# Loading q, k and v as plain rows, two-bank PSUM tiles, and transposing x pair by pair in a windowed attention followed by a soft mixture of experts

## The chip, the core and the metric

The kernel runs on one core of a Trainium2 chip. A core has five engines with instruction streams of their own: TensorE (PE in the profile; its weight loads are listed apart as PEld), VectorE (DVE), ScalarE (ACT), GpSimd (POOL) and SyncE (SP), and 16 DMA engines that move data between the chip's memory and the core's on-chip memories, SBUF and PSUM. Instructions on one engine run in order; engines wait for each other with semaphores. PSUM is where TensorE writes; it is used here in eight banks of 512 fp32 numbers per partition. The metric is device time in microseconds (us) for one execution. The kernel before took 291.89 us, the median of three runs between 289.92 and 292.55.

## The reference

Two layers, in fp32 in the reference (the kernel computes in fp16 with fp32 accumulation):

```python
# attention: q, k, v are (8 batches, 8 heads, 576 rows, 64)
scores = (q @ k.T) / 8
scores = where((0 <= i - j) & (i - j < 64), scores, -1e9)    # causal window of 64
attn   = softmax(scores)                                     # over j
x      = (attn @ v) -> transposed to (8*576 = 4608 tokens, 8*64 = 512)
# soft mixture of experts: phi (512, 8 experts * 4 slots), w1 (8, 512, 1024), w2 (8, 1024, 512)
logits = x @ phi                                             # (4608, 32)
d      = softmax(logits, over the 4608 tokens)
c      = softmax(logits, over the 32 slots)
slot_input = d.T @ x                                         # (32, 512)
slot_out   = relu(slot_input[e] @ w1[e]) @ w2[e]             # four slots per expert
out        = c @ slot_out                                    # (4608, 512), fp32
```

The expert layer can't start before all 4608 tokens have gone into `slot_input`, and the output can't start before the experts are done. So there are three stages: attention with the token side of the mixture, the experts, the output.

## The kernel before, in words

The order of all instructions is the order of the code (`manual_schedule`); tile pools add the waits for buffers. The unit of the first stage is a pair of heads of one batch: 8 x 4 = 32 pairs. The loop over `n` runs 36 times (32 pairs and `LAG` = 4), and each turn works on several pairs at different steps, so that an engine can have something from another pair:

- `st_transpose(n)`: the raw rows of q and k of pair n (tiles `qs`, `ks`) are turned on TensorE (L197, 24 transposes of 96 rows) into two banks, and ScalarE copies them to SBUF (L200), q with the scale 1/8.
- `st_score(n-3)`: a matmul with constants adds the mask and minus the row's maximum (L230, L233), matmuls add the scores (L242; the last 64 queries of each head go to a separate bank `sm`, L237 and L245), and ScalarE takes the exponential out of three banks (L248 twice, L249) into `pt`.
- `st_av(n-4)`: the weights times the values (L264, L266). Each value row has a column of ones beside it, so that the row sum comes out too. The result `av` has a two-bank PSUM tile of its own.
- `st_shift(n-2)`: the row maxima `m` are turned (L221, into the free end of `av`) and copied by VectorE to `rt` (L222), which the scores' constant matmul reads one turn later.
- `st_norm(n-4)`: VectorE takes reciprocals of the row sums (L274) and writes the normalised rows to `x_b` (L275).
- `st_max(n-1)`: the masked scores once more, with queries on the partitions (L207, L214), and VectorE's reduction to the row maxima `m` (L217), one bank per head.
- Of the batch two behind, one step per turn: in turns 0 and 1 `fr_transpose`, which turns x two pairs at a time (L291, L297; ScalarE copies, L293 and L298), in turn 2 `fr_logits` (L305; maxima, exponentials, running sums: `nb`, `lgT`, `d`, L310 to L325), in turn 3 `fr_dispatch` and `fr_slots` (`si`, L358 and L360, added to `acc`, L365). `fr_combine`, the softmax over slots, follows in the next turn (L334 to L342). The last batch's steps run one after the other behind the loop, and then the last two `fr_combine`.

PSUM holds six single banks that all steps share in turn (`bank`, pool `psum`), and the two-bank `av`.

The loads all stand in GpSimd's queue, whose instructions give the transfers to the DMA engines. At each batch's first turn: the batch's v in five transfers (L88, L90), the next batch's q and k (L79; two neighbouring rows of 64 go to one partition side by side, 96 partitions), and one expert's w1 and w2 (L62, L63). All inputs are fp32 in the chip's memory and are written to SBUF as fp16, so a row of 64 of q, k or v is 128 B when written, and two joined rows are 256 B. A value row has a pitch of 66 numbers, the ones column at 0 and the values at 1 to 64. A second copy of v, shifted by 64 rows, is made by two GpSimd copies in each batch's third turn (`shift_v`, L95, L96). A load has to wait for the last reader of the buffer that it overwrites, and the instructions behind it in GpSimd's queue wait with it. The eighth expert is loaded after the loop.

The tail: factors for the running softmax (L420 to L444), the slot inputs turned (L447, L449), the experts in two groups of four (first layer `hh` L458, transposes `th` L468, second layer `ops` L474), `osb` and `so4` (L479 to L483), then per batch five matmuls `cp` (L493) of up to 128 tokens each into one bank, copied to `ob` by ScalarE and VectorE in turn (L495, L497), and two output transfers per batch on SyncE's queue.

## Time and profile before

| | us, or as stated |
|---|---|
| median of three runs | 291.89 (289.92 to 292.55) |
| the profiled execution: span from the first to the last instruction | 285.9 |
| PE busy | 202.1 (71%), 4123 matmuls |
| VectorE busy | 142.4 (50%) |
| ScalarE busy | 133.2 (47%) |
| GpSimd busy | 99.6 (35%) |
| mean granted TensorE clock, 1 is full speed | 0.716 |
| DMA packets | 92,599, of them 75,664 under 512 B; 40.99 MB written |
| chain that ended last | PE 50%, DVE 13%, issue 10%, DMA 9%, ACT 9%, POOL 4% |

The profile is of one execution. Busy time is the time in which an engine has an instruction at work; "share" in a DMA column is the mean number of packets at work per DMA engine, so it can be above 1. In a row such as `tp<-ident_h,ks 96*64 96x96 f16 x384 | 18.9, 252 | 8.9` stand the output tile, the inputs, the shapes and how many there were; then the busy time in us, the mean of one in ns, and the idle time of the engine just before them, with what ended it. The page cuts the span into 40 slices of 7.15 us. Windows give the same for stretches that one chooses: start and end, length, then busy time and number of instructions of PE, PEld, DVE, ACT and POOL, granted clock, DMA share, and GB/s written. "The chain that ended last" is followed back from the last instruction: at each step to what released it. Its "issue" is time in which the engine waited for nothing that the profile shows.

### The profile page before, as it was taken

The page shows a single profiled execution, that of the slowest core. Times are in us where ns is not written, and L with a number is a line of the kernel's source. Part 1 is how long each engine was busy: PE and PEld are TensorE (multiplying, and loading weights), DVE is VectorE, ACT ScalarE, POOL GpSimd, SP SyncE. Part 2 cuts the span into 40 slices and gives each one's busy share as a digit, 9 for nine tenths or more (in the row PEclk, how much of TensorE's full clock was granted, in tenths as well). Part 3 has the DMA queues.
Part 4 walks back from the last instruction along what each step waited for, and adds up shares of the span by engine and source line. Part 5 has one row for each costly group of instructions (what it writes and reads, how often), then busy time and mean ns, then how long its engine had stood idle before and what let it go on. Part 6 is the DMA issues. An engine that isn't in the chain of part 4 may idle for free.

```text
span 285.9 us, 9168 instructions
## 1 busy us (share of the span) xinstructions
PE 202.1 (71%) x4123; PEld 131.1 (46%) x4123; DVE 142.4 (50%) x344; ACT 133.2 (47%) x279; POOL 99.6 (35%) x105
## 2 busy tenths in 40 slices
PE   0496875965797998599799968879866217777400
PEld 0264553743575755576475755567554003321000
DVE  4942632433663557257755537585773561155320
ACT  1353641670664466447647664583655201375210
POOL 7968127625563173509606542350020000000000
PEclk9999976695955558658855777796985555995555
DMA  7999999999999999999999999900009500029996
GB/s 75 153 134 203 192 107 196 204 113 161 210 151 133 204 178 106 187 189 99 135 205 175 108 197 196 91 5 2 2 9 190 96 1 2 0 97 338 353 333 203
DMA packets 92599, 40.99 MB, mean 143 GB/s; under 512 B 75664, under 2 KB 83856, under 8 KB 92560
## 3 DMA queue, kind: packets, MB, share of 16 engines
q0 software_dynamic: 87696, 30.97, 139.8%
q1 hardware_dynamic: 4864, 9.44, 9.8%
q8 instruction: 32, 0.52, 0.8%
q14 instruction: 7, 0.06, 0.1%
HBM read 61.93 MB, written 9.44 MB: 250 GB/s over the span
## 4 chain that ended last, share of the span: by engine, by line
PE 50%; DVE 13%; issue 10%; DMA 9%; ACT 9%; POOL 4%; DVEq 0%; POOLq 0%; ACTq 0%
PE sc L230 7%; PE tp L197 7%; PE mx L207 6%; PE av L264 6%; DMA out_dram<-ob 5%; DMA ks<-in_k_dram 5%; PE mx L214 4%; PE sc L242 3%; DVE m L217 3%; PE tx L291 2%; PE hh L458 2%; DVE ob L497 2%; PE sm L245 2%; PE av L221 2%; PE si L358 1%
## 5 line engine op out<-in xcount | busy, mean ns | idle before, releaser
L217 DVE TENSOR_REDUCE m<-mx 128x5 f16<-128x480 f32 x64 | 39.0, 652 | 8.7 <-PE mx L214 8.1
L88 POOL DMA_DIRECT2D v<-in_v_dram x32 | 28.3, 900 | 43.1 <-PE av L221 42.9
L222 DVE CAST rt<-av 10x128 f16<-10x128 f32 x32 | 9.2, 289 | 66.5 <-PE av L221 66.2
L248 ACT ACTIVATE pt<-sc 128x512 f16<-128x512 f32 x64 | 34.7, 601 | 15.3 <-PE sc L242 15.2
L200 ACT ACTIVATE qT<-tp 128x576 f16<-128x576 f16 x32 | 26.1, 816 | 24.6 <-PE tp L197 24.4
L230 PE MATMUL sc<-rt,lh 75*128 75x128 f16 x256 | 26.7, 264 | 7.3 <-issue 4.1
L207 PE MATMUL mx<-wm,ident_h 128*128 128x480 f16 x64 | 27.8, 516 | 3.0 <-issue 1.6
L200 ACT ACTIVATE kT<-tp 128x576 f16<-128x576 f16 x32 | 25.8, 805 | 7.5 <-PE tp L197 7.5
L293 ACT COPY xt<-tx 128x1024 f16<-128x1024 f16 x16 | 16.2, 1018 | 24.6 <-PE tx L291 24.6
L275 DVE TENSOR_TENSOR x_b<-av,rc 128x640 f16<-128x640 f32 x32 | 26.4, 824 | 1.1
L264 PE MATMUL av<-v,pt 128*64 128x65 f16 x576 | 21.6, 225 | 7.3 <-issue 6.6
L95 POOL COPY v<-v 64x2048 f16<-64x2048 f16 x8 | 15.2, 1906 | 32.1 <-DMA v<-in_v_dram 32.1
L197 PE MATMUL tp<-ident_h,ks 96*64 96x96 f16 x384 | 18.9, 252 | 8.9 <-DMA ks<-in_k_dram 5.0
L197 PE MATMUL tp<-ident_h,qs 96*64 96x96 f16 x384 | 19.1, 254 | 8.5 <-DMA qs<-in_q_dram 8.5
L214 PEld LDWEIGHTS <-qT 64*32 64x32 f16 x1152 | 12.3, 108 | 27.0 <-issue 26.2
L230 PEld LDWEIGHTS <-lh 75*128 75x128 f16 x256 | 19.6, 118 | 10.7 <-issue 6.0
L264 PEld LDWEIGHTS <-pt 128*64 128x64 f16 x576 | 17.0, 135 | 9.7 <-issue 7.2
L214 PE MATMUL mx<-kT,qT 64*32 64x96 f16 x1152 | 18.0, 251 | 4.1 <-issue 4.1
L197 PEld LDWEIGHTS <-qs 96*64 96x64 f16 x384 | 14.0, 141 | 13.8 <-DMA qs<-in_q_dram 8.5
L197 PEld LDWEIGHTS <-ks 96*64 96x64 f16 x384 | 15.3, 146 | 9.5 <-DMA ks<-in_k_dram 5.3
L497 DVE COPY ob<-cp 128x512 f32<-128x512 f32 (+1 forms) x20 | 12.4, 679 | 12.9 <-DMA out_dram<-ob 7.6
L318 ACT ACTIVATE d<-lg,nmax 128x128 f16<-128x128 f32 x8 | 2.9, 367 | 31.4 <-DVE lgT L314 31.4
(130 smaller groups left out, 351.4 us busy)
## 6 DMA issues: line engine op xcount, KB each, us to landing
w<-in_moe_w_dram POOLq DMA_DIRECT2D x16, 1024.0 KB, 18.5
out_dram<-ob SPq DMA_DIRECT2D x8, 1024.0 KB, 8.3
qs<-in_q_dram POOLq DMA_DIRECT2D x8, 576.0 KB, 11.5
ks<-in_k_dram POOLq DMA_DIRECT2D x8, 576.0 KB, 14.0
v<-in_v_dram POOLq DMA_DIRECT2D x32, 128.0 KB, 8.7
out_dram<-ob SPq DMA_DIRECT2D x8, 128.0 KB, 7.3
v<-in_v_dram POOLq DMA_DIRECT2D x8, 64.0 KB, 9.2
phi_sb<-in_moe_phi_dram POOLq DMA_DIRECT2D x1, 32.0 KB, 7.9
```

What stands on the lines that cost most here:

```text
L88: nc.gpsimd.dma_start(out=v1[:, :, c, 1:65], in_=v[b, :, 128 * c:128 * c + 128, :].rearrange("h p d -> p h d"))
L197: nc.tensor.transpose(tp[64 * hl:64 * hl + 64, j, GP * c:GP * c + GP], src[:, GC * (2 * hp + hl) + c, Dh * j:Dh * j + Dh], ident_h[0:GP, 0 ...
L200: nc.scalar.activation(dst.rearrange("p (g j) -> p j g", j=RQ), tp[:, :, :], AF.Copy, scale=sc)
L207: nc.tensor.matmul(mx[hl][:, :, :], ident_h[:, :], wm[:, :, :], start=True, stop=False, skip_group_check=True)
L214: nc.tensor.matmul(mx[hl][32 * t:32 * t + 32, c, :], qT[r, o:o + 32], kT[r, o:o + 96], start=False, stop=True, skip_group_check=True)
L217: nc.vector.reduce_max(m[:, 5 * hl:5 * hl + 5], mx[hl][:, :, :], axis=AXX)
L230: nc.tensor.matmul(sc[hl][:, 2 * c:2 * c + 2, :], lh[:, 5 * hl + c, :], rt[:, :], start=(c == 0), stop=False, skip_group_check=True)
L248: nc.scalar.activation(pt[:, 9 * hl:9 * hl + 8, :], sc[hl][:, :, :], AF.Exp)
L264: nc.tensor.matmul(av[r0:r0 + 64, hl, 65 * (i // 2):65 * (i // 2) + 65], pt[:, 9 * hl + i, :], rhs, start=True, stop=True)
L275: nc.vector.tensor_tensor(out=x_b[:, :, 128 * hp:128 * hp + 128].rearrange("p c (l d) -> p l c d", l=2), in0=avv[:, :, :, 1:65], in1=rc[:, ...
L293: nc.scalar.copy(out=xt[:, 2 * k2:2 * k2 + 2, 0:512], in_=tx[:, :, :])
L497: nc.vector.tensor_copy(out=ob[0:pn, t, :], in_=cp[0:pn, :])
```

## The change

The change is made all over the kernel. What is computed stays the same.

- **Loads.** q, k and v of a batch are each loaded in one transfer as plain rows: the 8 x 576 rows of a batch in order, 128 to a chunk, 36 chunks (`flat`, `NCH`). Every row is written as 128 B. Value rows now have a pitch of 96 numbers (192 B), values at 0 to 63, the ones column at 64 (`VP`). An odd head begins in the middle of a chunk. The shifted copy of v is made by VectorE, in a batch's fourth turn.
- **Order of the loads.** Ahead of the loop: q and k of batch 0 in two parts, v 0, q and k of batch 1, w1 and w2 of expert 0. Then v of the batch and q and k of the next at each batch's first turn, and one half of an expert (w1 or w2) in the turns of a list (`WSLOTS`). The eighth expert goes into the freed buffers of q and k at turn 32 (`load_last`). phi is loaded on SyncE's queue as fp32 and converted by VectorE.
- **PSUM.** Four two-bank tiles serve all steps in turn (`banks`): `tp` (q and k turned, beside them the `sm` scores and the turned dispatch weights), `sc`, `av`, `mx` and `f` (the turned x of one pair, and the logits or slot sums). One instruction empties both banks where two did before: the maxima's reduction and the large exponential.
- **x.** `fr_transpose` turns one pair per turn (five transposes, one copy) instead of two pairs in each of two turns. Logits follow in the turn after the last pair, slots one turn later.
- **fr_combine** is cut in two, one turn apart; the last one is placed among the experts.
- **Tail.** Both groups' first layers run ahead of the transposes and second layers; the output is copied from two banks at a time and sent in three transfers per batch.

The order of TensorE's work in a turn is: transposes of pair n, (dispatch transposes), scores of n-3, values of n-4, shift of n-2, maxima of n-1, (logits), x of n-5, (slots). The core of the diff:

```diff
+    NRES = E - 1
+    NCH = H * S // 128
+    VP = 96
...
-    psum = ctx.enter_context(tc.tile_pool(name="psum", bufs=6, space=bass.MemoryType.PSUM))
-    pav = ctx.enter_context(tc.tile_pool(name="pav", bufs=1, space=bass.MemoryType.PSUM))
-
-    def bank(shape, dt, name):
-        return psum.tile(shape, dt, name=name, tag="ps")
-
-
-    w1_t, w2_t = {}, {}
-
-    def load_expert(e, pool):
-        w1_t[e] = pool.tile([128, NKK, F], FP16, name=f"w1_{e}")
-        w2_t[e] = pool.tile([128, NFC, D], FP16, name=f"w2_{e}")
-        nc.gpsimd.dma_start(out=w1_t[e], in_=moe_w1[e].rearrange("(c p) f -> p c f", p=128))
-        nc.gpsimd.dma_start(out=w2_t[e], in_=moe_w2[e].rearrange("(c p) d -> p c d", p=128))
-
-    att = ExitStack()
-    pin = att.enter_context(tc.tile_pool(name="pin", bufs=2))
-    pqk = att.enter_context(tc.tile_pool(name="pqk", bufs=1))
-    pvv = att.enter_context(tc.tile_pool(name="pvv", bufs=1))
-    pw = att.enter_context(tc.tile_pool(name="pw", bufs=2))
-    pxb = att.enter_context(tc.tile_pool(name="pxb", bufs=2))
-    pxt = att.enter_context(tc.tile_pool(name="pxt", bufs=1))
+    psum = ctx.enter_context(tc.tile_pool(name="psum", bufs=4, space=bass.MemoryType.PSUM))
+    pin = ctx.enter_context(tc.tile_pool(name="pin", bufs=2))
+    def banks(name):
+        t = psum.tile([128, 2, 512], FP32, name=name, tag="ps")
+        return t, t[:, :, :].bitcast(FP16)
+    def flat(src, b):
+        return src[b].rearrange("h s d -> (h s) d").rearrange("(c p) d -> p c d", p=128)
...
-    def load_qk(b):
-        qs = pin.tile([GP, H * GC, RQ * Dh], FP16, name="qs", tag="qs")
-        ks = pin.tile([GP, H * GC, RQ * Dh], FP16, name="ks", tag="ks")
-        for t_, src in ((qs, q), (ks, k)):
-            nc.gpsimd.dma_start(out=t_, in_=src[b].rearrange("h (c g j) d -> g (h c) (j d)", g=GP, j=RQ))
...
-            nc.gpsimd.dma_start(out=v1[:, :, c, 1:65],
-                                in_=v[b, :, 128 * c:128 * c + 128, :].rearrange("h p d -> p h d"))
-        nc.gpsimd.dma_start(out=v2[64:128, :, 4, 1:65],
-                            in_=v[b, :, 512:576, :].rearrange("h p d -> p h d"))
...
-        nc.gpsimd.tensor_copy(out=v2[0:64, :, 1:5, 1:65], in_=v1[64:128, :, 0:4, 1:65])
-        nc.gpsimd.tensor_copy(out=v2[64:128, :, 0:4, 1:65], in_=v1[0:64, :, 0:4, 1:65])
...
+    def new_qk(b):
+        staged[b] = tuple(pin.tile([128, NCH, Dh], FP16, name=n, tag=n) for n in ("qs", "ks"))
+    def load_qk(b, c0=0, c1=NCH):
+        for t_, src in zip(staged[b], (q, k)):
+            nc.gpsimd.dma_start(out=t_[:, c0:c1, :], in_=flat(src, b)[:, c0:c1, :])
+    new_qk(0)
+    load_qk(0, 0, 9)
...
+    load_qk(0, 9, NCH)
...
+    def load_w(i):
+        e, second = divmod(i, 2)
+        if second:
+            nc.gpsimd.dma_start(out=w2_t[e, 0], in_=w2_dram(e))
+        else:
+            nc.gpsimd.dma_start(out=w1_t[e, 0], in_=w1_dram(e))
+    def load_last(half):
+        e = E - 1
+        a = pin.tile([128, 2, F], FP16, name="w1h", tag="qs")
+        c = pin.tile([128, 4, D], FP16, name="w2h", tag="ks")
+        nc.gpsimd.dma_start(out=a, in_=w1_dram(e)[:, 2 * half:2 * half + 2, :])
+        nc.gpsimd.dma_start(out=c, in_=w2_dram(e)[:, 4 * half:4 * half + 4, :])
+        w1_t.setdefault(e, []).extend(a[:, i, :] for i in range(2))
+        w2_t.setdefault(e, []).extend(c[:, i, :] for i in range(4))
...
+    v1s = [pvv.tile([128, NCH, VP], FP16, name=f"v1_{i}") for i in range(2)]
+    v2s = [pvv.tile([128, NCH, VP], FP16, name=f"v2_{i}") for i in range(2)]
+    def load_v(b):
+        nc.gpsimd.dma_start(out=v1s[b % 2][:, :, 0:Dh], in_=flat(v, b))
+    def shift_v(b):
+        v1, v2 = v1s[b % 2], v2s[b % 2]
+        nc.vector.tensor_copy(out=v2[64:128, :, 0:Dh], in_=v1[0:64, :, 0:Dh])
+        nc.vector.tensor_copy(out=v2[0:64, 1:NCH, 0:Dh], in_=v1[64:128, 0:NCH - 1, 0:Dh])
+    load_v(0)
+    new_qk(1)
+    load_qk(1)
+    load_w(0)
+    load_w(1)
...
+        c0 = 9 * hp
+        even = [(0, 128, c0 + c, 128 * c) for c in range(4)] + [(0, 64, c0 + 4, 512)]
+        odd = [(64, 128, c0 + 4, 0)] + [(0, 128, c0 + 5 + c, 64 + 128 * c) for c in range(4)]
+        for w, src in enumerate(staged[b]):
+            for parts in zip(even, odd):
+                for hl, (r0, r1, c, o) in enumerate(parts):
+                    nc.tensor.transpose(tq[64 * hl:64 * hl + 64, w, o:o + r1 - r0], src[r0:r1, c, :],
+                                        ident_h[r0:r1, r0:r1])
+    def st_copy(p, tq):
+        qk = qkT[p % NQ]
+        nc.scalar.activation(qk[:, 0, 64:64 + S], tq[:, 0, 0:S], AF.Copy, scale=scale)
+        nc.scalar.copy(out=qk[:, 1, 64:64 + S], in_=tq[:, 1, 0:S])
...
+        mx, _ = banks("mx")
...
+        nc.vector.reduce_max(m[:, :].rearrange("p (l c) -> p l c", l=2),
+                             mx[:, :, 0:480].rearrange("p l (c x) -> p l c x", x=96), axis=AXX)
...
+        sc, _ = banks("sc")
+        sm = tp[:, :, 288:352]
...
+    def st_exp(p, sc, sm):
+        pt = pts[p]
+        nc.scalar.activation(pt[:, :, 8, :], sm[:, :, :], AF.Exp)
+        nc.scalar.activation(pt[:, :, 0:8, :].rearrange("p l i x -> p l (i x)"), sc[:, :, :], AF.Exp)
...
+        for c in range(5):
+            n = 128 if c < 4 else 64
+            nc.tensor.transpose(fq[:, 0, 128 * c:128 * c + n], x_b[0:n, c, 128 * hp:128 * hp + 128], ident_h[0:n, 0:n])
+        nc.scalar.copy(out=xts[b][:, hp, :], in_=fq[:, 0, 0:S])
...
+        return lambda: fr_combine2(b, ec, rs, cc)
+    def fr_combine2(b, ec, rs, cc):
...
+    WSLOTS = {5: 2, 9: 3, 11: 4, 13: 5, 17: 6, 19: 7, 21: 8, 25: 9, 27: 10, 28: 11, 29: 12, 30: 13}
     LAG = 4
+    pending = {}
+    for n in range(NP + LAG + 1):
+        kb, ph = divmod(n, HP)
+        if ph == 0 and n > 0:
+            if kb < B:
+                load_v(kb)
+            if kb + 1 < B:
+                new_qk(kb + 1)
+                load_qk(kb + 1)
+        if n in WSLOTS:
+            load_w(WSLOTS[n])
+        if n == 32:
+            load_last(0)
+            load_last(1)
+        sb = (n - 10) // HP if n >= 10 and (n - 10) % HP == 0 else None
+        lb = (n - 9) // HP if n >= 9 and (n - 9) % HP == 0 else None
+        cb = (n - 11) // HP if n >= 11 and (n - 11) % HP == 0 else None
+        tp = tq = sc = None
+        if n < NP or 0 <= n - 3 < NP or sb is not None:
+            tp, tq = banks("tp")
         if n < NP:
+            st_transpose(n, tq)
+        if sb is not None:
+            fr_dispatch(sb, tq)
         if 0 <= n - 3 < NP:
+            sc, sm = st_score(n - 3, tp)
+        if n < NP:
+            st_copy(n, tq)
+        if sb is not None:
+            fr_dispatch_copy(sb, tq)
+        if sc is not None:
+            st_exp(n - 3, sc, sm)
+        av = None
+        if 0 <= n - 4 < NP or 0 <= n - 2 < NP:
+            av, _ = banks("av")
         if 0 <= n - 4 < NP:
             st_av(n - 4, av)
         if 0 <= n - 2 < NP:
             st_shift(n - 2, av)
+            st_shift_copy(n - 2, av)
         if 0 <= n - 4 < NP:
             st_norm(n - 4, av)
+        if ph == 3 and kb < B:
+            shift_v(kb)
+        if n == 5:
+            late_constants()
         if 0 <= n - 1 < NP:
             st_max(n - 1)
+        f = None
+        if 0 <= n - 5 < NP or lb is not None or sb is not None:
+            f, fq = banks("f")
+        if lb is not None:
+            lg = fr_logits(lb, f)
+        if 0 <= n - 5 < NP:
+            fr_transpose(n - 5, fq)
+        if lb is not None:
+            fr_exp(lb, lg)
+        if sb is not None:
+            si = fr_slots(sb, f)
+            fr_acc(sb, si)
+        if sb is not None:
+            pending[sb] = fr_combine(sb)
+        if cb is not None:
+            pending.pop(cb)()
...
+    f, _ = banks("f")
+    fr_exp(B - 1, fr_logits(B - 1, f))
+    tp, tq = banks("tp")
+    fr_dispatch(B - 1, tq)
+    fr_dispatch_copy(B - 1, tq)
+    f, _ = banks("f")
+    fr_acc(B - 1, fr_slots(B - 1, f))
+    pmid.close()
...
+    ha, _ = banks("ha")
+    first_layer(0, ha)
+    hb, _ = banks("hb")
+    first_layer(1, hb)
+    tht, th = banks("tht")
+    hidden_transpose(0, th)
+    finish = fr_combine(B - 1)
+    op, _ = banks("op")
+    second_layer(0, op[:, 0, :])
+    hidden_transpose(1, th)
+    second_layer(1, op[:, 0, :])
+    finish()
...
+        for t0 in (0, 2, 4):
+            cp, _ = banks("cp")
+            ts = (t0, t0 + 1) if t0 < 4 else (4,)
+            for i, t in enumerate(ts):
+                pn = 128 if t < 4 else 64
+                r = slice(32 * t, 32 * t + 32) if t < 4 else slice(96, 128)
+                o = 0 if t < 4 else 128
+                nc.tensor.matmul(cp[0:pn, i, :], ct_all[r, b, o:o + pn], so4[r, :], start=True, stop=True,
+                                 skip_group_check=True)
+            pn = 128 if t0 < 4 else 64
+            dst, src = ob[0:pn, t0:t0 + len(ts), :], cp[0:pn, 0:len(ts), :]
+            if turn % 2 == 0:
+                nc.scalar.copy(out=dst, in_=src)
             else:
+                nc.vector.tensor_copy(out=dst, in_=src)
+            turn += 1
+            if t0 < 4:
+                r0 = 576 * b + 128 * t0
+                nc.sync.dma_start(out=out[r0:r0 + 256, :].rearrange("(c p) d -> p c d", p=128),
+                                  in_=ob[:, t0:t0 + 2, :])
+            else:
+                nc.sync.dma_start(out=out[576 * b + 512:576 * b + 576, :], in_=ob[0:64, 4, :])
```

## The prediction

> **What bounds the kernel now.** I read the page first, its slices and its DMA queues:
>
> ```profile
> PEclk9999976695955558658855777796985555995555
> DMA  7999999999999999999999999900009500029996
> GB/s 75 153 134 203 192 107 196 204 113 161 210 151 133 204 178 106 187 189 99 135 205 175 108 197 196 91 5 2 2 9 190 96 1 2 0 97 338 353 333 203
> q0 software_dynamic: 87696, 30.97, 139.8%
> q8 instruction: 32, 0.52, 0.8%
> ```
>
> A slice is 7.15 us. The DMA engines are full until slice 25 (186 us), and the rate swings between about 105 and 205 GB/s. The instruction queue moves 32 packets, 0.52 MB: 16 KB each.
>
> Then the windows, the first five chosen so that one kind of load, or two that meet, can be told apart, the last one a whole batch:
>
> ```profile
> 5.00:10.00 5.00, 0.69 (x12) 0.50 (x12) 4.43 (x15) 0.76 (x1) 4.62 (x12) 1.00 1.82 181
> 108.00:113.00 5.00, 5.00 (x131) 3.28 (x127) 3.92 (x10) 2.89 (x7) 1.77 (x3) 0.82 3.96 90
> 122.00:126.00 4.00, 4.00 (x100) 2.51 (x96) 3.08 (x7) 1.04 (x3) 0.00 (x0) 0.50 1.19 207
> 179.00:182.00 3.00, 2.35 (x55) 1.74 (x56) 1.60 (x3) 1.86 (x6) 2.19 (x3) 0.91 1.93 127
> 182.00:185.00 3.00, 3.00 (x75) 1.77 (x70) 1.53 (x4) 1.51 (x4) 0.00 (x0) 0.53 2.97 77
> 105.00:131.00 26.00, 21.92 (x484) 15.72 (x478) 13.43 (x33) 14.54 (x31) 10.42 (x11) 0.65 2.09 151
> ```
>
> The last two columns are the DMA share (above 1: packets of one engine overlap) and GB/s written. q and k, 256 B written per packet, run at 181 (5:10). Weights run at 207 (122:126). v, 128 B per packet, alone in 179:185, starts at 127 and falls to 77 while the share rises from 1.93 to 2.97: its writes pile up. Where the end of v meets the next q and k (108:113) both crawl at 90 with a share of 3.96. In the batch window PE is busy for 21.9 of 26 us, DVE and ACT for 13.4 and 14.5.
>
> Then the chain that ended last, around that crawl:
>
> ```profile
> 112.73 0.54 PE mx L207 x2
> 113.28 0.23 PE mx L214 x19
> 113.51 3.73 issue
> 117.23 0.40 PE mx L214 x15
> ```
>
> PE stops in the middle of a run of equal matmuls, waiting for no other engine. Such pauses stand at 34.8 (1.66), 41.8 (4.09), 62.2 (5.64), 87.4 (1.60), 113.5 (3.73), 139.4 (2.01) and 163.1 (0.62), 19.4 us by 180: one per batch, most of them while q and k follow v. With 16 KB instruction packets on the same DMA engines I read them as late instruction fetches.
>
> So PE bounds the attention loop, with a pause per batch that the DMA crawl makes, at a clock that is often half. The first q transposes (L197) of batches 1 to 7 stand at 26.1, 49.4, 77.5, 104.5, 131.5, 155.5 and 180.3 us; the first 26 us wait for the k of batch 1. The six batches between take 154.2 us, 25.7 each.
>
> **The change, part by part.** I count from the span, 285.9 us; the median run of 291.9 is 6.0 more, which I take as fixed around the span.
>
> *Loads.* q, k and v now all come as 4608 packets of 128 B per batch and tensor, so q and k go from 2304 to 4608 packets. Values go to rows at 192 B, before at 132 B and 2 B off. A load's 0.59 MB takes 3.3 us at 181 GB/s, 4.65 us at 127, 7.7 us at 77. No row shows an aligned 128 B write alone. I take 127, what v itself does before its writes pile up: nearest in size, and without the offset, I argue, the pile need not form, since 256 B packets never piled up when alone. A weight half (1.05 MB at 207) takes 5.05 us; 1.5 of them per batch until iteration 28 instead of 2. DMA per batch: 3×4.65 + 1.5×5.05 = 21.5 us, below the 25.7 of today. POOL's queue loses the 1.9 us copies (L95, L96) and four of five v issues: DMAs only wait for PE's last use of their buffer, as before.
>
> The Trainium skill speaks against this: "DMA: Bandwidth & Descriptors", Specifications, gives 512 B as the least transfer for line rate and says that smaller ones are read-modify-written. The trace disagrees at 256 B (181 GB/s, share steady) and leaves 128 B open; by that rule the slow end of the loads, 7.7 us, would hold for q and k too. This is the third rival.
>
> *Start.* Five loads stand ahead of iteration 4: 4.0 us to the first packets (estimated from issue at 1.3 and landing at 8.5) + 5×4.65 = 27.3 against 26.1; with its first transposes 28. **+2.**
>
> *Pauses.* If the crawl goes, the pause goes: 19.4/6 = 3.2 us per batch. **−19.4.** Next late is PE itself at 22.5 us per batch, with DMA at 21.5 just under it.
>
> *PE.* 20 transposes of up to 128 columns for 24 of 96: 24×96 and 16×128+4×64 are equal columns, 1.10 us at half clock. One sm matmul fewer per pair. Pair-wise x transposes: the same 20 per batch. 0, ±0.2 us per iteration (±6).
>
> *Merged evacuations.* m 652 ns at 480 elements against nb's 362 at 192 gives 168 ns fixed, so merging saves 32×0.17 = 5.4 us of DVE; exp (601 at 512, 299 at 128) gives 198 fixed, 6.3 us of ACT. Both idle half of each window: 0, a gain only if PE ran at full clock throughout. The ring of four two-bank tiles: transposes of n+1 take the scores' tile of n, free after 0.82+0.80+0.30+1.0 = 2.9 us of ACT; PE needs 1.1+0.45+0.15+1.0+0.4 = 3.1 us at full clock (110 to 114 us in the timeline) to come back. No wait, barely.
>
> *shift_v on DVE.* Not shown in this form. lh<-mb moves 1280 in 0.67 us, lh<-db 1280 in 1.21: 2304 elements are 1.2 to 2.2 us, twice per batch. I take 2.4 in all: a plain copy, as lh<-mb. It stands ahead of the reduce that frees the tile for the next av. DVE: 0.29+0.22+0.82+2.4+1.14 = 4.9 us after av; PE returns to av after 4.9 at half clock, 3.1 at full. **+1.0 per batch, +6** (0 to +11). It also waits for v on DVE, with the reduce, and through it PE, queued behind. v is issued three iterations (17 us) ahead and lands within 10 (5.05 backlog + 4.65): covered.
>
> *Logits.* nb now also waits for ACT's copy of x (about 0.66 us) and ACT for nb; today ACT waits 31.4 us there in 8 times and PE is not held. 0 (to +5).
>
> *From iteration 28 on.* Batch 7 and the drain keep their 23.0 and 13.1 us. x^T is copied per pair: instead of 3.4 us from x_b to the last logits' start (217.1 to 220.5) about 1.7. **−1.7.** The two combines on DVE (226.06 to 231.05) leave the path: one inside the loop, one beside the experts. **−4.9.** The experts (13.3 us, 237.75 to 251.03) run as 3.6+2.6+0.5+0.85+1.9+0.4+0.85+1.9 = 12.6. **−0.7.** First output DMA after one 1.0 us copy of two banks instead of four alternating ones, 254.64 to about 253.9: **−0.7**; then 9.4 MB at about 340 GB/s as before. Expert 7's load was not on the path (hh waited for ACT's sit), so moving it wins 0; it now lands near 210, first needed after 220.
>
> Sum: +2 −19.4 +6 −1.7 −4.9 −0.7 −0.7 = −19.4; span 266.5, time **272**.
>
> **The rivals.**
> 1. *Faster: the clock stays up too.* Without pauses PE may keep full clock, where iterations took 4.1 us (161.4 to 165.5, 185.3 to 189.4). At 5.0 us a batch is 20, or 21 with the shift; DMA must keep up (3.6 us loads). 6×(25.7−21) = 28 and 3 in batch 7, plus 8: 39 off, 253. Against: 79 to 105 us ran at clock 0.50 with PE busy for 23.9 of 26 us.
> 2. *The pauses stay.* They come from any long run of small packets, of which there are now more. Batches stay at 25.7+1: +2 +6 −8 = 0: 292. The Trainium skill ("Runtime: NRT & Kernel Launch", Instruction fetch mechanics) calls fetch mostly hidden behind execution; then the pauses were never fetches and nothing here removes them. The instruction packets near each pause's end speak against it.
> 3. *Slower: 128 B is slow as such.* Place: DMA. If a load takes over 6.0 us (98 GB/s), 3 loads + 7.6 exceed 25.7 and PE waits at each batch's first transposes. At 6.6 us: batches 27.4, iteration 4 at 37: +11 +10 −8 = +13, 305. At 7.7: batches 30.7, +16 +30 −8 = +38, 330. For: 77 and 90 GB/s. Against: that v is both unaligned and small, and starts at 127.
>
> **How the numbers follow.** Forecast 0.45 (262 to 282, by the ± of PE, shift and logits); clock 0.23 (247 to 262); pauses stay 0.14 (284 to 297); 128 B slow 0.18 (295 to 330). 252 to 303 leaves out some 0.08 below and 0.12 above. One per cent is about what the three runs (289.9 to 292.6) can tell. Faster by over 1% (under 289): 0.45+0.23+0.05 = 0.73; within: 0.08; slower: 0.19.
>
> **What would show it.** Right: windows in which q and k run near 127 GB/s or above with a share near 2, DMA slices below 9 somewhere before 180 us, chain pauses ("issue") under 5 us in all, batch 7's first transposes near 168, no combine between acc and the tr matmuls. Wrong: a share of 3 to 4 through q, k and v (rival 3), transposes waiting for qs or ks in every batch, issue pauses as before (rival 2), av waiting for the reduce at each fourth iteration (shift underpriced), or a clock that falls as PE is fed less evenly.

## The result and the profile after

The changed kernel is slower: 305.22 us, the median of four runs (300.53 to 310.60), against 291.49 for the kernel before in the same runs. The ratio is 1.038, with a 95% interval of 1.029 to 1.047. Two of the four runs were slower ones at a lower granted clock, and this ratio, like all ratios below, is of the fast runs alone, so it is smaller than that of the medians. The forecast was 272. The profiled execution spans 298.8 us, 12.9 more than before.

These lines of its page answer to those shown of before (granted clock, DMA share and rate in 40 slices, now of 7.47 us; the queues of loads):

```profile
PEclk9999999998599579957995597797588555796555
DMA  8999999999599809997990999099990000008997
GB/s 62 157 147 192 189 156 171 72 156 201 97 92 158 134 2 140 171 207 56 157 178 5 135 167 213 12 154 211 208 206 12 2 0 0 3 2 306 357 355 246
q0 software_dynamic: 123584, 30.94, 123.4%
```

The DMA engines are no longer full all the time: there are slices with 5, 8 and 0, and slices at 2, 5 and 12 GB/s before the loop's end. The loads move 123,584 packets instead of 87,696, and their packets take less time in all, 123% of the engines' span instead of 140%.

Two windows: v, q and k alone, and one batch. The columns are those of the prediction, the last three granted clock, DMA share and GB/s.

```profile
36.00:44.00 8.00, 8.00 (x120) 5.23 (x118) 4.53 (x18) 3.74 (x7) 0.00 (x0) 1.00 2.53 158
111.00:138.00 27.00, 24.60 (x475) 15.55 (x472) 17.25 (x33) 13.50 (x28) 7.72 (x6) 0.81 1.75 146
```

The 128 B rows load at 158 GB/s with no crawl; 0.59 MB take 3.7 us. But PE is busy for 24.6 of 27 us, at a granted clock of 0.81, where before it was busy for 21.9 of 26 at 0.65. The loop got more TensorE work, not more waiting. Where it sits is seen in the chain that ended last: start, length, and how many matmuls. First the changed kernel, each row the whole block that turns q and k of one pair, at the slow and the fast matmul rate:

```profile
55.11 2.41 PE tp L223 x20
62.45 1.67 PE tp L223 x20
```

Then the kernel before, the same block at the fast and the slow rate:

```profile
30.93 0.79 PE tp L197 x24
40.16 1.10 PE tp L197 x24
```

Twenty transposes take twice as long as twenty-four did. The waits of TensorE (for whom, us in all, times, longest) show the other side: the pauses with no wait shown ("issue"), 20.1 us in 9 in the kernel before by the same view, are nearly gone, and a new wait stands first. Before:

```profile
PE av L264 <- issue: 6.6, 3, 5.6
PE sc L230 <- issue: 4.1, 1, 4.1
PE mx L214 <- issue: 4.1, 2, 3.7
PE tx L291 <- issue: 2.0, 1, 2.0
PE tp L197 <- issue: 1.7, 1, 1.7
PE mx L207 <- issue: 1.6, 1, 1.6
```

After:

```profile
PE tp L379 <- ACT d L348: 9.5, 8, 2.6
...
PE f L332 <- issue: 1.1, 1, 1.1
PE f L324 <- issue: 1.0, 1, 1.0
```

By stages: the first block of batch 1 stands at 26.4 us (26.1 before, though that is its k half; its q half stood at 23.3) and that of batch 7 at 193.2 (180.3), so a batch takes 27.8 us instead of 25.7. From there to the last `x_b` it is 44.5 us instead of 36.1, and from that to the end 61.1 instead of 69.5.

The starts of the matmuls in the block that begins at 62.4 us, read from the trace, in ns from the first one, with the rows that each takes (64-row ones marked h):

```
q: 0  173h  316 320  397 400  453 456  605h  749
k: 752 925h  1069 1071  1149 1152  1205 1208  1357h  1500
```

Two 128-row transposes that write to the two halves of the output partitions start 3 ns apart; the next pair follows after some 53 to 78 ns. At every step between a 128-row and a 64-row one, 143 to 173 ns pass. There are eight such steps in a block.

### The profile page after: what moved, and what is told of

Same layout as the page of the kernel before. It is cut to its first block, busy times and chain, and to the rows that moved or that the text cites. A ratio compares the mean times of both kernels' runs of the same rounds, so it can differ in the third digit from the quotient of the medians.

```text
span 298.8 us, 8723 instructions
## 1 busy us (share of the span) xinstructions
PE 236.5 (79%) x3963; PEld 142.0 (48%) x3963; DVE 160.5 (54%) x326; ACT 124.7 (42%) x245; POOL 63.6 (21%) x57
## 3 DMA queue, kind: packets, MB, share of 16 engines
q0 software_dynamic: 123584, 30.94, 123.4%
## 4 chain that ended last, share of the span: by engine, by line
PE 62%; DVE 15%; ACT 8%; DMA 6%; issue 3%; POOL 1%; DVEq 0%; SPq 0%; ACTq 0%; POOLq 0%
PE tp L223 15%; PE sc L271 7%; PE mx L236 7%; PE f L324 5%; PE av L297 5%; PE mx L243 4%; PE sc L276 4%; ACT xt L325 3%; DMA out_dram<-ob 3%; DMA ks<-in_k_dram 3%; DVE v L146 2%; PE av L251 2%; DVE m L246 2%; PE tp L263 2%; DVE x_b L309 2%
## 5 line engine op out<-in xcount | busy, mean ns | idle before, releaser
L223 PE MATMUL tp<-ident_h,qs 128*64 128x128 f16 (+1 forms) x320 | 37.1, 258 | 7.8 <-DMA qs<-in_q_dram 7.8
L228 ACT ACTIVATE qkT<-tp 128x576 f16<-128x576 f16 x32 | 20.8, 650 | 53.3 <-PE tp L267 38.7
L141 POOL DMA_DIRECT2D v<-in_v_dram x8 | 14.5, 1817 | 127.8 <-PE av L251 127.1
L325 ACT COPY xt<-f 128x576 f16<-128x576 f16 x32 | 20.4, 637 | 45.6 <-PE f L324 45.6
L223 PE MATMUL tp<-ident_h,ks 128*64 128x128 f16 (+1 forms) x320 | 37.7, 263 | 1.7 <-DMA ks<-in_k_dram 1.7
L246 DVE TENSOR_REDUCE m<-mx 128x10 f16<-128x960 f32 x32 | 36.8, 1151 | 1.6 <-PE mx L243 1.2
L285 ACT ACTIVATE pt<-sc 128x1024 f16<-128x1024 f32 x32 | 33.0, 1031 | 4.0 <-PE sc L276 2.2
L223 PEld LDWEIGHTS <-qs 128*64 128x64 f16 (+1 forms) x320 | 22.1, 121 | 21.3 <-DMA qs<-in_q_dram 8.0
L223 PEld LDWEIGHTS <-ks 128*64 128x64 f16 (+1 forms) x320 | 22.4, 123 | 12.2 <-issue 2.5
L309 DVE TENSOR_TENSOR x_b<-av,rc 128x640 f16<-128x640 f32 x32 | 26.4, 824 | 1.1
L271 PE MATMUL sc<-rt,lh 128*128 128x128 f16 x256 | 26.6, 267 | 0.2 <-ACT xt L325 0.2
L236 PE MATMUL mx<-wm,ident_h 128*128 128x480 f16 x64 | 26.2, 505 | 0.0
L229 ACT COPY qkT<-tp 128x576 f16<-128x576 f16 x32 | 20.3, 633 | 0.0
```

What stands on the lines that cost most here:

```text
L223: nc.tensor.transpose(tq[64 * hl:64 * hl + 64, w, o:o + r1 - r0], src[r0:r1, c, :], ident_h[r0:r1, r0:r1])
L228: nc.scalar.activation(qk[:, 0, 64:64 + S], tq[:, 0, 0:S], AF.Copy, scale=scale)
L236: nc.tensor.matmul(mx[:, hl, 0:480], ident_h[:, :], wm[:, :, :].rearrange("p c x -> p (c x)"), start=True, stop=False, skip_group_check=True)
L246: nc.vector.reduce_max(m[:, :].rearrange("p (l c) -> p l c", l=2), mx[:, :, 0:480].rearrange("p l (c x) -> p l c x", x=96), axis=AXX)
L271: nc.tensor.matmul(sc[:, hl, 128 * c:128 * c + 128], lh[:, 5 * hl + c, :], rt[:, :], start=(c == 0), stop=False, skip_group_check=True)
L285: nc.scalar.activation(pt[:, :, 0:8, :].rearrange("p l i x -> p l (i x)"), sc[:, :, :], AF.Exp)
```

## The experiments

### The order of the transposes

Theory: TensorE stops when the number of rows changes. Rivals: 128-row transposes are slow as such, or something else sets the pace. One edit to the changed kernel:

```diff
-        for w, src in enumerate(staged[b]):
-            for parts in zip(even, odd):
+        full = list(zip(even[0:4], odd[1:5]))
+        half = [(even[4], odd[0])]
+        for w, group in ((0, full), (1, full), (0, half), (1, half)):
+            for parts in group:
```

> The changed kernel with one edit: of the 20 transposes of q and k in a turn, the 16 that take all 128 rows come first and the four that take 64 rows last. Nothing is added or removed. In the changed kernel's trace two neighbouring 128-row transposes start 3 ns apart, but at each step between a 128-row and a 64-row one 143 to 173 ns pass; there are 8 such steps in the block, which takes 1.67 us at full clock and 2.41 at half, against 0.79 and 1.10 for before's 24. Theory, steps between row counts stop TensorE: 6 of 8 steps go, 6 x 0.11 us at full and 6 x 0.16 at half clock, so the block takes about 1.0 and 1.4, and 32 turns save 21 to 31 us of TensorE time; some of it turns into waits, so the time falls by 15 to 30 us against the changed kernel's 305. Rival 1, a 128-row transpose is slow in itself: block and time unchanged within 1%. Rival 2, VectorE (the shifted copy of v, then the reduction) or the loads set the pace: the block gets shorter but the time stays within 1% of 305.

Measured: 281.8 us, 0.976 of before (0.961 to 0.990). That is 23 us below the changed kernel by the medians, and 18 by the two ratios (0.062 of 291): the theory, and neither rival. The chain shows the block at the fast rate:

```profile
67.61 0.74 PE tp L225 x20
```

From the first to the last start the block takes 0.62 us at the fast and 1.07 at the slow rate, where it took 1.50 and 2.17: seven steps fewer inside it, 0.126 and 0.157 us each. A dose between the two, in the order `(0, full), (0, half), (1, full), (1, half)`:

> A dose between the changed kernel and a1_grouped: q's eight 128-row pairs, q's 64-row pair, then the same for k, so 3 steps between row counts inside the block of 20 transposes instead of 8 (changed kernel) or 1 (a1_grouped). From the first to the last start the block takes 1.50 us at full and 2.17 at half clock with 8 steps, 0.62 and 1.07 with one. Theory, each step costs the same, 0.126 and 0.157 us: 0.87 and 1.38 us with 3. Rival, only the pairs of unequal transposes (one of 128 and one of 64 rows) are slow, and here there are none: 0.62 and 1.07.

It takes 0.84 and 1.33 us with three steps, 0.11 and 0.13 us for each of the two added: the price is per step, within a fifth. Its one run took 282.2 us.

Next the two other places where the change had added such steps:

```diff
         for hl in range(2):
+            for c in range(4):
+                nc.tensor.matmul(sc[:, hl, 128 * c:128 * c + 128], lh[:, 5 * hl + c, :], rt[:, :],
+                                 start=(c == 0), stop=False, skip_group_check=True)
+        for hl in range(2):
             r = slice(64 * hl, 64 * hl + 64)
             nc.tensor.matmul(sm[:, hl, :], qk[r, 1, 512:640], qk[r, 0, 576:640],
                              start=False, stop=True, skip_group_check=True)
-        for hl in range(2):
-            for c in range(4):
-                nc.tensor.matmul(sc[:, hl, 128 * c:128 * c + 128], lh[:, 5 * hl + c, :], rt[:, :],
-                                 start=(c == 0), stop=False, skip_group_check=True)
...
-            n = 128 if c < 4 else 64
-            nc.tensor.transpose(fq[:, 0, 128 * c:128 * c + n], x_b[0:n, c, 128 * hp:128 * hp + 128], ident_h[0:n, 0:n])
+            nc.tensor.transpose(fq[:, 0, 128 * c:128 * c + 128], x_b[:, c, 128 * hp:128 * hp + 128], ident_h[:, :])
```

> The one before this in the list, and two more edits that take steps between row counts away: the constant matmuls of the scores come before the 64-row score matmuls of sm (three steps become one), and the fifth transpose of x takes all 128 rows instead of 64, with 64 columns that nobody reads (two steps fewer). Theory, steps stop TensorE: four more steps per turn, 4 x 0.11 to 0.16 us, less 0.03 to 0.05 for the added columns, so another 0.4 to 0.6 us per turn and 12 to 19 us of TensorE time, 8 to 18 us of the time if TensorE still sets the pace. Rival, something else bounds the turn once the block is short: no further change over 1%.

277.5 us (0.961, 0.951 to 0.971): 4.4 less, about half of what was expected, and the two intervals overlap. At the fast rate the score block does get shorter, from 1.07 to 0.86 us, and the five transposes of x from 0.33 to 0.23. But TensorE's busy time falls by 5.7 us in all (192.7 to 187.0), not by 12 to 19, and ten of its blocks of q and k stand at the slow rate, where `a1_grouped` has six; why isn't settled. TensorE waits 14.9 us in 8 times for `d` here and 5.1 for the shifted v, nearly as in `a1_grouped` (15.1 and 4.1), where the changed kernel had 9.5 and none.

The converse, planted in the kernel before:

```diff
-        for hl in range(2):
-            for c in range(4):
+        for c in range(4):
+            for hl in range(2):
                 nc.tensor.matmul(sc[hl][:, 2 * c:2 * c + 2, :], lh[:, 5 * hl + c, :], rt[:, :],
                                  start=(c == 0), stop=False, skip_group_check=True)
+            for i in (2 * c, 2 * c + 1):
+                for hl in range(2):
+                    r = slice(64 * hl, 64 * hl + 64)
+                    nc.tensor.matmul(sc[hl][:, i, :], kT[r, 64 * i:64 * i + 128], qT[r, 64 * i:64 * i + 64],
+                                     start=False, stop=True, skip_group_check=True)
...
-        for i in range(8):
-            for hl in range(2):
-                r = slice(64 * hl, 64 * hl + 64)
-                nc.tensor.matmul(sc[hl][:, i, :], kT[r, 64 * i:64 * i + 128], qT[r, 64 * i:64 * i + 64],
-                                 start=False, stop=True, skip_group_check=True)
```

> The converse, on the kernel before: the same 29 matmuls of the scores in another order, each two constant matmuls (75 rows) followed by the four 64-row score matmuls of the same columns, so 9 steps between row counts in a turn's score block instead of 1; nothing else is touched, neither loads nor PSUM. In before's trace the block takes 0.98 us at full and 1.66 at half clock from its first to its last start. Theory, a step costs 0.126 and 0.157 us wherever it stands: 8 more make the block 2.0 and 2.9 us, TensorE works 32 to 40 us more, and as it sets the pace of the loop the time rises by 20 to 35 us. Rival, the steps cost only in transposes, or only between transposes of unequal width: block and time as before, within 1%.

305.3 us (299.2 to 306.7) against 290.8 (288.3 to 294.9): 14 us more by the medians, 11 between the fastest runs, from the order of the same matmuls alone. The block takes 1.82 us at the fast and 2.57 at the slow rate, from 0.98 and 1.66: 0.105 and 0.114 us per step. PE's busy time rises from 202.1 to 239.3 us, as expected, but the time by less than the 20 expected at least: the pauses shrank from 20.1 to 8.0 us at the same time. So steps cost in ordinary matmuls too, and part of what TensorE loses shows up as shorter pauses.

### Loads

Is it the offset of v that made the crawl, and the crawl that made the pauses? The kernel before, with the value rows as in the changed one:

```diff
-    v1s = [pvv.tile([128, H, 4, 66], FP16, name=f"v1_{i}") for i in range(2)]
+    v1s = [pvv.tile([128, H, 4, 96], FP16, name=f"v1_{i}") for i in range(2)]
...
-            nc.gpsimd.dma_start(out=v1[:, :, c, 1:65],
+            nc.gpsimd.dma_start(out=v1[:, :, c, 0:64],
```

> The kernel before with one edit: value rows at a pitch of 192 B with the values at 0 and the ones column at 64, as in the changed kernel, instead of 132 B with the values 2 B off. Theory, the offset makes v's 128 B writes pile up, and the pile-up makes TensorE's pauses: v's packets then keep 150 to 160 GB/s as in the changed kernel, the share stays near 2, the pauses shrink from 19 us in all to under 5, and the time falls from 291 by 10 to 19 us. Rival, the pauses have another cause (the five small transfers, the instruction stream itself): the rate of v rises but the time stays within 1%.

273.5 us, 0.947 (0.938 to 0.955). The windows of v alone and of the q and k behind it, where before fell to 77 and 90 GB/s with a share of 3 to 4:

```profile
31.00:34.00 3.00, 3.00 (x81) 1.93 (x80) 2.03 (x5) 1.18 (x4) 0.39 (x1) 1.00 2.13 160
36.00:40.00 4.00, 2.21 (x72) 1.49 (x72) 2.46 (x5) 2.24 (x5) 2.30 (x2) 1.00 1.88 181
```

160 GB/s for v, 181 for q and k, a share near 2: the crawl came from how v's rows lay, 2 B off and at a pitch of 132 B. The edit changes both, and no run tells them apart; "offset" stands for both below. The pauses fall to 9.5 us, though not under 5. This one edit of the change, alone, is worth 15.5 us.

The other load edit alone, single rows of q and k beside the offset v (`RQ = 1` for `RQ = 2` in the kernel before):

> The kernel before with one edit: q and k as single rows, 128 B written per packet, 4608 packets per load instead of 2304; v stays at its offset. Theory, a 128 B write is not slow as such: q and k load at about 157 GB/s, 3.8 us instead of 3.3, 1 us more DMA per batch, and as loads are waited for only at the start the time stays within 1% (start +1 us). Rival, 128 B rows pile up beside weights and values whatever their place: q and k crawl at 77 to 100 GB/s, the pauses grow and the time rises by over 3%.

305.5 us, 1.058 (1.050 to 1.065): the rival, as far as time and pauses go. The windows are those in which v and the next q and k run side by side:

```profile
40.00:46.00 6.00, 4.06 (x112) 2.80 (x113) 2.98 (x7) 2.55 (x5) 1.65 (x2) 0.82 4.88 87
66.00:72.00 6.00, 1.94 (x58) 1.55 (x53) 0.72 (x2) 3.21 (x7) 1.16 (x2) 0.93 4.90 83
```

More small packets stand beside the offset rows, the share goes to 4.9, and the pauses to 31.2 us. That the offset rows slow their neighbours shows in single packets: in the kernel before, a 256 B packet of q or k takes 41 ns in the median without v (115 to 117.8 us) and 113 to 142 ns beside it (109 to 113 us), and a 128 B packet of v there 120 to 149, against 32 in `b_valign`. Both load edits together:

> The kernel before with both load edits: aligned value rows (b_valign) and q and k as single 128 B rows (b_rq1). b_rq1 alone cost 5.8% and its q and k fell to 64 to 104 GB/s beside the offset v; b_valign alone gained 5.3%. Theory, only the offset rows of v are slow, and what they slow is every small packet beside them: q, k and v all load at about 157 GB/s, 1 us per batch more than in b_valign, and the time is that of b_valign, 273, plus 0 to 4 us. Rival, single 128 B rows cost by their number whatever v does: the time is b_valign's plus 14 or more.

284.1 us (0.985, 0.973 to 0.998): 10.7 above `b_valign`, between the theory and its rival. About 5 us of it are waits for q and k, 16.9 us against 11.6 in all, mostly at the start. Single rows do cost something by their number here.

### The shifted copy of v, and the dispatch

```diff
-        if ph == 3 and kb < B:
+        if ph == 2 and kb < B:
             shift_v(kb)
```

> The kernel with all three orders mended (a2_allorder) and one edit: the shifted copy of v in a batch's third turn instead of its fourth, still on VectorE. In the traces of the changed kernel and of a2_allorder the two copies take 0.75 us each where GpSimd issues no transfer, but 1.2 and 1.97 where it issues the next v, q and k at the same time; in the fourth turn both wait for the same av, so they meet in every batch. Theory, VectorE's copies are slowed by GpSimd's issues: in the third turn both copies take 0.75 us, 1.7 us per batch less on VectorE, TensorE's wait for the copy (5.1 us in 5 times) goes, and the time falls by 6 to 14 us against a2_allorder. Rival, the copies are slow for their 64-partition shift or for the pitch: 1.2 and 1.97 us stay, and the time stays within 1%.

268.5 us (0.929, 0.912 to 0.947), 9.0 below `a2_allorder`. The two copies in the changed kernel (shortest, median, longest in ns):

```profile
L145 DVE COPY v<-v x8: 742/1167/1221, 25.3 to 220.1; 64x2304 f16<-64x2304 f16 x8
L146 DVE COPY v<-v x8: 752/1968/1970, 26.1 to 220.8; 64x2240 f16<-64x2240 f16 x8
```

and in this kernel:

```profile
L145 DVE COPY v<-v x8: 742/752/755, 18.6 to 182.0; 64x2304 f16<-64x2304 f16 x8
L146 DVE COPY v<-v x8: 752/753/1986, 19.4 to 182.8; 64x2240 f16<-64x2240 f16 x8
```

They take 0.75 us each but for one, and that one, at 19.4 us, follows another into an issue on GpSimd (L141). In the changed kernel six of eight pairs met the issues of v and of q, k or weights, because the issues wait for the last `av` that reads the buffer, and the copies stand behind the `x_b` that waits for the same `av`. Every slowed copy in these two traces ends 0.55 or 0.56 us after the end of an issue. The edit also puts the copies a turn earlier; how much of the 9.0 us comes from that and how much from their length, no run tells apart.

The Trainium skill, "SBUF — State Buffer", Who interferes with whom, says that VectorE's copies in their fast form and GpSimd's instructions share a pair of ports, and that the one that starts first blocks the other for its whole length. That fits: 0.75 us alone, 1.97 behind an issue; and at 18.6 us in `c1_shift`, where the copy took its 0.74 us inside an issue, that issue lasted 2.58 us instead of 1.82.

The dispatch transposes behind the scores, and their copies behind the exponentials:

```diff
-        if sb is not None:
-            fr_dispatch(sb, tq)
         if 0 <= n - 3 < NP:
             sc, sm = st_score(n - 3, tp)
+        if sb is not None:
+            fr_dispatch(sb, tq)
```

> The kernel a2_allorder with one edit: the transposes of the dispatch weights (td, L380 and L381) stand behind the scores in TensorE's order, and their copies behind the exponentials in ScalarE's, instead of ahead of them. In a2_allorder TensorE waits 14.9 us in 8 times there for ScalarE's d, with the scores queued behind. Theory, this wait holds the turn: inside the loop 7 x 1.8 us of it are covered by the scores (about 1.6 us at full clock), so the time falls by 5 to 12 us. Rival, the same chain over VectorE and ScalarE (copy of x, maxima, exponentials) ends last anyway and TensorE waits somewhere else in the turn: within 1%.

272.9 us (0.948, 0.936 to 0.959), 4.5 below `a2_allorder`: just under the expected range, and the intervals overlap. TensorE's wait for `d` at that place (L380) falls to 6.9 us. Both edits:

> The edits of c1_shift and c2_dispatch together on a2_allorder. Theory, they take away two different waits, one at a batch's fourth turn and one at the turn after its logits: the gains add up, 9.0 and 4.5 us off 277.5, so about 264. Rival, both give back the same slack to the same chain: no better than c1_shift's 268.5 within 1%.

264.9 us (0.924, 0.911 to 0.937): about the 264 of the theory, and 3.6 us below `c1_shift`, but the intervals overlap, so that the gains add up isn't shown beyond noise. This kernel beats both the one before and the changed one, with the changed kernel's instructions but for a few columns in the transposes of x, in another order.

### What is left of the forecast's other terms

```diff
-        nc.vector.reduce_max(m[:, :].rearrange("p (l c) -> p l c", l=2), ...
+        for hl in range(2):
+            nc.vector.reduce_max(m[:, 5 * hl:5 * hl + 5], ...
```

and the same for the exponential:

> The kernel c3_both with the merged evacuations undone: the reduction to the maxima and the large exponential one bank at a time, two instructions each again, the two-bank tiles kept. Theory of the prediction, both engines have slack: within 1%. Rival, in the turns that are left after the mended orders VectorE and ScalarE stand in the chain: 32 x 0.17 and 32 x 0.2 us come back on it, 4 to 11 us.

266.4 us (259.6 to 267.1) against 264.9 (264.6 to 268.0): no difference that these runs can tell; the rival's 11 us are excluded, its 4 not strictly. Then before's loads of q and k (two rows joined) in `c3_both`:

> The kernel c3_both with before's loads of q and k: two rows joined, 256 B per packet, 2304 packets per load, 24 transposes of 96 rows, and copies that put the rows back in order; the shifted copy of v gets a pitch of 144 B instead of 192 to make room. Theory, single rows cost by their number at the start, where the loads are waited for, and by late loads and pauses after it (b_rq1_valign stood 10.7 us above b_valign): joined rows give 4 to 10 us back against c3_both. Rival, in the loop the loads are covered and the pauses were already gone in the changed kernel (16 us of gaps on TensorE from 25 to 230 us, two of them with no wait shown): only the start moves, by 1 to 4 us, and ScalarE's copies, 0.81 us for 0.64, take it back: within 1%.

263.2 us (0.913, 0.896 to 0.929) against 0.924: 1.7 us, within 1%, so the rival. TensorE's waits for q and k are 11.6 us instead of 15.0. Why single rows cost 10.7 us in the older order of work and hardly anything here isn't settled.

Last, the pauses, which come back in `c3_both`: 16.0 us in 10, with no crawl. Two kernels leave loads out, the first those of q, k and v from batch 2 on, the second the weights' too, but for the first and the last expert (its last hunk).

```diff
-            if kb < B:
+            if kb == 1:
                 load_v(kb)
             if kb + 1 < B:
-                new_qk(kb + 1)
-                load_qk(kb + 1)
+                staged[kb + 1] = staged[(kb + 1) % 2]
...
-        if n in WSLOTS:
-            load_w(WSLOTS[n])
```

> The kernel c3_both without the loads of q, k and v from batch 2 on: later batches compute on the data of batches 0 and 1 that are still in place, so the output isn't the reference's; all else, the weights' loads too, stays. By the waits with no releaser on TensorE the pauses are 20.1 us in the kernel before, 9.5 in b_valign, 2.1 in the changed kernel, 8.0 in b_steps and 16.0 in c3_both: they shrink with the crawl, but also wherever TensorE is slower. Theory, small packets on the DMA engines delay the instruction fetch: without them the pauses fall under 5 us. Rival, TensorE in the short turn takes its instructions faster than they come, whatever the DMA engines do: 10 us or more stay. A third, the weights' large packets delay it as much: 5 to 10 us stay, all while weights load.

> The same without the weights' loads in the loop too: all experts but the last use the weights of expert 0, so the output isn't the reference's. From about 35 us on no load runs until the last expert's. Theory, loads delay the fetch: pauses under 2 us. Rival, TensorE outruns the fetch by itself: as many as in f1_noqkv, 10 us or more.

One run each, 253.9 and 245.7 us. The pauses are 7.2 us in the first, the third of the cases, and the four of over 1 us in the chain stand between 47 and 80 us, while weights still load. In the second, this is the only row of its kind among TensorE's waits:

```profile
PE sc L280 <- issue: 0.4, 1, 0.4
```

So loads make the pauses, small packets and large ones, and TensorE by itself hardly outruns its instructions.

The traces also tell what a pause is. Queue q8 moves, by its count, TensorE's instructions: its 31 or 32 packets of 16 KB are one for every 256 or so matmuls and weight loads. They land 5 to 7 us apart in the median. Each of the 117 pauses that this view gives in the 16 traces ends 1.2 to 2.0 us after one of these packets has landed. In the kernel before, the longest one (5.6 us) ends at 67.8 us, and its packet landed at 66.2. So the pauses are late instruction fetches.

The Trainium skill, "Runtime: NRT & Kernel Launch", Instruction fetch mechanics, calls the fetch mostly hidden. The runs agree where no load is under way (0.4 us in `f2_noloads`) and not beside loads (16.0 in `c3_both`, 20.1 in the kernel before).

## Why the prediction was wrong

**The step that failed is the one on PE:** "20 transposes of up to 128 columns for 24 of 96 ... are equal columns, 1.10 us at half clock." The columns are equal; the block takes 2.41 us. The four transposes of 64 rows, at which an odd head begins in the middle of a chunk, make eight steps between row counts in each turn. By the blocks, 32 turns x 0.88 (1.67 less 0.79) to 1.31 us (2.41 less 1.10) are 28 to 42 us of TensorE, of which mending the order gave back 18 to 23 in the time, and the two other places 4.4. The bound of ±6 had no row behind it that changes rows. Such a row was in the trace of before: its two constant matmuls of `sm` (L233, 75 rows) start 29 ns apart in the median, and the 64-row one behind them (L237) 149 ns after the second. That is about 0.12 us per step; eight in each of 32 turns make 31 us.

The Trainium skill has the rule: "TensorEngine Tiling (Array Packing)", Key Properties, says that changing the tiling mode, and not just the tile, drains TensorE. It spoke against this change and the prediction didn't weigh it. The traces agree, with 0.105 to 0.157 us per step between row counts, and, in the kernel before, with a stop between matmuls of equal rows and other columns: from L242 (64 rows, 128 columns of weights) to L245 (64 rows, 64 columns) it is 119 to 169 ns, where two of L242 start 22 ns apart in the median.

Without most of these steps (`a2_allorder`) the kernel takes 277.5 us, inside the forecast's own range of 262 to 282. That is in part luck, as other terms were off too: with the shifted copy and the dispatch mended as well it is at 264.9. The other steps, one by one:

- **Loads and start: right in kind.** No crawl once v is aligned; 158 GB/s, better than the 127 taken, and no sign of the third rival's slow end of 7.7 us; first block of batch 1 0.4 us later, not 2.
- **Pauses: the size came out, partly by luck.** 20.1 us became 2.1, nearly the −19.4. Aligning v alone takes away 10.6 us of pauses. The rest went because TensorE got slower: `b_steps`, with the old crawl, has 8.0 instead of 20.1, and as the order is mended they come back, 5.6 us in `a1_grouped`, 8.2 in `a2_allorder`, 16.0 in `c3_both`. A pause is a late packet of instructions met by a TensorE that is otherwise quick, so "next late is PE itself at 22.5 us per batch" counted as pure gain what a faster TensorE meets again. That they are late instruction fetches, as the prediction read them, holds.
- **Shifted copy: the price was off.** +6 (0 to +11) was taken for 2.4 us of plain copies. They cost 3.1 us in most batches (1.17 and 1.97) and 1.5 where GpSimd is quiet; making them short and a turn earlier moved the time by 9.0, inside the bound.
- **Logits: the upper end.** 0 (to +5) was costed; TensorE waits 9.5 us there, and `c2_dispatch` makes it 4.5 us of time, with intervals that overlap. ACT's wait of 31.4 us there before held nobody, but in the new order TensorE's scores queue behind it.
- **Merged evacuations: right** as far as `e1_split` shows, no change that can be told.
- **From `x_b` of the last pair to the end: right.** −8.0 forecast, 69.5 to 61.1 us measured, −8.4. But "batch 7 and the drain keep their 23.0 and 13.1 us" fell with the turn: 44.5 instead of 36.1.
- **The rivals.** The third one gave 305 at 6.6 us a load, and 305.2 was measured; that is a coincidence. Its mechanism needs over 6.0 us, a load took 3.7, and DMA slices were empty. Its evidence, 77 and 90 GB/s, belonged to the offset rows. The first one's clock did rise (0.716 to 0.799) and the second one's pauses went, but neither decided the time.

## What to carry to other kernels

Count the changes between 64-row and taller tiles in a stream of TensorE work, not only its columns: here each cost 0.10 to 0.16 us, eight per turn cost 6 to 8% of the time, and putting equal ones together gave it back without touching a single operand. Place a VectorE copy where GpSimd isn't issuing transfers; a wait that both share put them on top of each other in most batches here. When a stall vanishes, look whether its cause went or whether the engine that suffered only got slower, since a later improvement will bring it back.

## What the runs showed of the hardware that had not been expected

- A step between 64-row matmuls and those of 75 or 128 rows stops TensorE for 0.105 to 0.157 us, at either matmul rate, in transposes and in plain matmuls. In the kernel before, a step from 128 to 64 columns of weights at equal rows does it too (119 to 169 ns from start to start).
- Writing 128 B rows 2 B off, at a pitch of 132 B, slows the loads near them too: 77 to 90 GB/s, against 158 to 160 aligned, and 113 to 142 ns for a 256 B packet beside them, against 41.
- VectorE copies of 64 x 2304 and 64 x 2240 fp16 take 0.75 us each alone, and 1.0 to 2.0 behind GpSimd's issues of transfers.
- TensorE's pauses follow its instruction packets: all 117 of them end 1.2 to 2.0 us after a 16 KB packet of queue q8 has landed, and they shrink to 0.4 us when no loads run.
- The granted clock isn't the whole matmul rate. In this window of the changed kernel it is 1.00 and PE is busy throughout,

```profile
14.00:62.00 48.00, 48.00 (x747) 29.33 (x747) 24.79 (x58) 18.58 (x31) 17.01 (x12) 1.00 2.24 155
```

yet equal matmuls (L236) start 372 ns apart throughout, and 213 at 66 us. In `a1_grouped`, with shorter blocks of transposes, the first at 212 stands at 22 us, and most after it are at 212 or 213. What decides it stays open. The Trainium skill, "TensorE: Matmul & The Clock Gate", Seeing it yourself, warns that the recorded clock events have been seen to be unreliable, which fits.
